# Fused Nyström attention and two feed-forward layers on one Trainium2 core: weight conversions loaded one ahead of their arithmetic, token blocks of the next tile begun two quartets later

## The chip, the core and the metric

The kernel runs on one core of a Trainium2 chip (trn2). The metric is the device time of one launch in microseconds (us). Below, TensorE is called PE, VectorE DVE, ScalarE ACT, GpSimd POOL and SyncE SP, as the profile calls them. All loads and stores of this kernel are issued from SP.

## What is computed

Inputs arrive as 64-bit floats. An attention block with landmarks feeds two feed-forward layers:

```python
A, Bm, C = sm(q, k_lm), sm(q_lm, k_lm), sm(q_lm, k)     # 4 batches, 8 heads, 576 tokens, 32 landmarks
x = (A @ Z @ C @ v)                                     # Z: six Newton steps towards the inverse of Bm
h = x @ w_in;  x = (h * clip(h + 3, 0, 6) / 6) @ w_out  # 2304 tokens, 512 -> 2048 -> 512
h = x @ w2_in; x = elu(h) @ w2_out                      # the same sizes
```

## The kernel before

**Stages.** The first feed-forward layer is worked in 128 slots (`NA`): four batches, two halves of a batch, 16 slices of the hidden width. Slot i multiplies into the hidden slice (`slot_a1`), applies the gate on ACT and DVE, and three slots later multiplies back (`slot_a2`). The attention of the next batch, its matmuls included, is worked between the slots. The second layer is worked in 24 quartets: three tiles of 768 tokens, eight quartets a tile. A quartet has seven block products (`quartet`, the seven blocks stand for eight by a Strassen-like scheme) and the products back to the output (`second`), which follow eight blocks behind.

**Conversions.** The weights of the second layer come as 64-bit floats and must become 32-bit floats before the quartets. That is done by 32 conversions, 16 of `w_out` (`conv_out2`, line 351) and 16 of `w_in` (`conv_in2`, line 354), one in every second slot from slot 36 (`O2`, line 1197). Each calls `to_dram` (line 291): SP loads 512 KB into a tile `u`, ACT makes the number (`y<-u`, line 226) and scales the low word (`u<-u`, line 228), DVE shifts and puts in the sign (`y<-y`, line 232, and `y<-u,y`, line 237), POOL adds the low word (`y<-y,u`, line 241), and SP stores `y` (256 KB) to a scratch buffer in DRAM. `to_dram` issues the load, then `flush` issues the store of the conversion before, then comes the arithmetic. There are three `u` buffers (`UB`) and two `y` buffers (`YB`). The `u` buffers also serve as scratch elsewhere (`scratch`, line 358).

**Token blocks.** For a tile t the second layer needs 14 sums and differences of blocks of the first layer's output, each split into a high and a low part. `load_x(t)` (line 534) is a generator of 24 steps; the loop calls one step per block of a quartet, so that a tile takes 24/7 = 3.4 quartets. For tile 0 it runs in the last slots (line 1202, on DVE), for tiles 1 and 2 it starts in quartet 1 and quartet 9 (`XPACE`, line 1233), with its subtractions on POOL (`xf<-xf,x`, `xf<-x,xf`, `x<-xf,x`, `x<-x`) and its copies on ACT. Its work tiles `xf` take the places of `ath0`, `ath1` and `atl0`, which hold the attention operand of the first layer and later the output rows `ob`.

**Weights of a quartet.** `load_in2` and `load_out2` load the converted weights, split them (`wi<-wi`, `wi<-u,wi`, `w<-w` on POOL; eight small sums and differences `u<-u,wi`, `u<-wi,u` on DVE) and, in the first tile, store the split form for the later tiles.

**What sets the order.** Each engine works its own queue strictly in order. The order in a queue is not that of the program text: a scheduler lays it down when the kernel is built. `wanted(s)` gives the instructions that follow it a due number, counted in slots (a quartet counts as four). `gated` binds the load of a conversion to come, in the schedule, behind the matmuls of the slot before. `flow` keeps the arithmetic of the conversions in their own order on each engine. In the second layer `bmm` fixes the order of the matmuls by hand.

The calls around the change are these:

```python
        if (i - END) % O2 == 0 and conv:
            gate[0] = marks["slot"]
            wanted(i + 4)
            conv.pop(0)()
            gate[0] = None
...
        if q % NQ == XPACE and q // NQ + 1 < NTT:
            xs = load_x(q // NQ + 1, pool)
...
            wanted(NA + 4 * q + 4 * p / 7 + 4)
            if conv and p % 2 == 0:
                conv.pop(0)()
            next(xs, None)
```

Of the kernel before, what the change touches and what calls it, by code (L numbers as in the profile page):

```python
# [10 lines left out]
F32 = mybir.dt.float32  # L11
# [20 lines left out]
def nystrom_ffn_kernel(ctx: ExitStack, tc, q, k, v, w_in1, w_out1, w_in2, w_out2, out):  # L32
# [49 lines left out]
    W = 512  # L82
# [10 lines left out]
    YB, UB, SE = 2, 3, 1  # L93
    PRE, NLEAD, EI, EO = 2, 2, 3, 4
    GATE1, O2, NEW1 = 8, 2, 0
    PACE, NEW, PACE1 = 0.5, -4, 0.2
    XSET, XPACE = 4, 1
    NAT = 25, 28, 31

    strict = [False]  # L100
# [23 lines left out]
    vec, act, pool, pe = InOrder(nc.vector), InOrder(nc.scalar), InOrder(nc.gpsimd), InOrder(nc.tensor)  # L124
# [9 lines left out]
    stg = ctx.enter_context(tc.tile_pool(name="stg", bufs=2, reuse_waits="tile"))  # L134
# [16 lines left out]
    def wanted(s):  # L151
        tc.cur_priority = int(1000 * (s + 100))
# [11 lines left out]
    def gated(inst):  # L164
        if gate[0] is not None:
            after(inst, gate[0])
# [38 lines left out]
    def flow(eng, inst):  # L205

        if not strict[0] and eng.flow is not None:
            after(inst, eng.flow)
        eng.flow = inst.ins

    def steps(src, u, f, out=None):

        if len(src.shape) == 3:
            gated(sp.dma_start(
                out=u.rearrange("p n t -> p (n t)"), in_=src.rearrange("p k n -> p (k n)").bitcast(U32)
            ))
            u = u.rearrange("p (k n) t -> p k n t", k=src.shape[1])
            lo, hi = u[:, :, :, 0], u[:, :, :, 1]  # L220
        else:
            gated(sp.dma_start(out=u.rearrange("p n t -> p (n t)"), in_=src.bitcast(U32)))
            lo, hi = u[:, :, 0], u[:, :, 1]
        fi = f.bitcast(U32)
        yield act, 0
        flow(act, act.activation(out=f, in_=hi.bitcast(F32), func=AF.Copy, scale=2.0 ** -112))
        yield act, 0
        flow(act, act.activation(out=lo, in_=lo, func=AF.Copy, scale=2.0 ** -29))
        yield vec, 1

        t = fi if between[0] is None else between[0].bitcast(U32)
        flow(vec, vec.tensor_scalar(
            out=t, in0=fi, scalar1=3, scalar2=0x7FFFFFFF, op0=ALU.logical_shift_left, op1=ALU.bitwise_and
        ))
        if between[0] is None:
            yield vec, 1
        flow(vec, vec.scalar_tensor_tensor(
            out=fi, in0=hi, scalar=0x80000000, in1=t, op0=ALU.bitwise_and, op1=ALU.bitwise_or
        ))
        yield pool, 1  # L240
        flow(pool, pool.tensor_tensor(out=fi if out is None else out.bitcast(U32), in0=fi, in1=lo, op=ALU.add))

    def run(gen):
        for _ in gen:
            pass
# [32 lines left out]
    def room(tag=None):  # L278
        if tag:
            return nat.tile([128, W, 2], U32, name="un", tag=tag)  # L280
        return stg.tile([128, W, 2], U32, name="u", tag="u", bufs=UB)

    pending = []

    def flush():

        while pending:
            o, i = pending.pop(0)
            sp.dma_start(out=o, in_=i)

    def to_dram(o, src, k=1):

        u = room()
        y = stg.tile([128, W], F32, name="y", tag="y", bufs=YB)
        gen = steps(src, u, y.rearrange("p (k n) -> p k n", k=k) if k > 1 else y)
        next(gen)
        flush()
        run(gen)
        pending.append((o, y))

    def to_pair(f, h, l, eng=vec):
        act.copy(out=h, in_=f)
# [48 lines left out]
    def conv_out2(kk):  # L351
        to_dram(wo2d[kk], part(w_out2, kk, 0))

    def conv_in2(m, kk):

        to_dram(wi2d[m, kk], w_in2[m, kk], 4)
# [321 lines left out]
    def newton(b):  # L678

        EB, sb, sc, cvs = newton_tiles()  # L680
        s = [SB * (b - 1) + (NEW if b > 1 else NEW1)]
        kept = {}

        def go(gen, n=99):
            for _ in range(n):
                wanted(s[0])
                try:
                    s[0] += next(gen) * (PACE if b > 1 else PACE1)
                except StopIteration:
                    return  # L690

        def keep(key, gen):
            kept[key] = yield from gen

        go(prep(b, 0))
        go(score_b(b, 0, sb, EB))
        go(keep(0, score_c(b, 0, sc)))
        go(soft(b, 0))
        go(values(b, 0, kept[0], cvs))
        go(prep(b, 1))  # L700
        go(score_b(b, 1, sb, EB))
        inv = keep("Q", inverse(EB, sb))
        sC = keep(1, score_c(b, 1, sc))
        sA = soft(b, 1)
        go(inv, 1)
        go(sC, 2)
        go(inv, 1)
        go(sC)
        go(inv, 2)
        go(sA, 3)  # L710
        go(inv, 2)
        v1 = values(b, 1, kept[1], cvs)
        go(v1, 2)
        go(inv, 2)
        go(sA)
        go(v1)
        go(inv)
        go(finish(b, kept, cvs, sc))
# [75 lines left out]
    def attn_at(b, hf, eng=pool):  # L794

        s, n = span(b, hf)
        ath = nat.tile([128, G, n], F32R, name="ath", tag=f"ath{hf}")
        atl = nat.tile([128, G, n], F32R, name="atl", tag=f"atl{hf}")
        for g in range(G):
            at = ft.tile([128, T2], F32, name="at", tag="at" if g or b or hf else "gf", bufs=1 if g or b or hf else 2)[:, 0:n]  # L800
            vec.transpose(out=at, in_=e_t[b, g][:, s // 32:(s + n) // 32, :].rearrange("p t l -> p (t l)"))
            yield
            act.copy(out=ath[:, g, :], in_=at)
            sub(atl[:, g, :], at, ath[:, g, :].bitcast(F32), eng)
        at_t[b, hf] = (ath, atl)

    def attn_n(b, c, n=W):

        nh = nat.tile([128, G, W], F32R, name=f"nh{c}", tag=f"nh{c}")
        nl = nat.tile([128, G, W], F32R, name=f"nl{c}", tag=f"nl{c}")  # L810
        n_t[b, c] = (nh, nl)
        w1 = w1_t[b, c]
        mt = mt_t[b]
        for o in range(0, W, n):

            nps = [bank()[:, 0:n] for _ in range(G)]
            for j in range(4):
                for g in range(G):
                    p0 = 64 * g
                    inst = mm(nps[g][32 * j:32 * j + 32, :], mt[p0:p0 + 64, j, :],  # L820
                              w1[p0:p0 + 64, o // 128:(o + n) // 128, j, :], True, True)
                    ordered(inst)
                    if b > 1 and g == j == 0:
                        after(inst, marks["slot"])
                        after(inst, prev[0])
            if b > 1:
                hold[0] = last[0]
            for g in range(G):
                h, l = nh[:, g, o:o + n], nl[:, g, o:o + n]
                act.copy(out=h, in_=nps[g])  # L830
                sub(l, nps[g], h.bitcast(F32))
            yield
        nb, nc_ = (b, c + 2) if c + 2 < NW else (b + 1, c + 2 - NW)
        if 0 < nb < B:
            load_w1(nb, nc_)
# [341 lines left out]
    conv = [lambda kk=kk: conv_out2(kk) for kk in range(NKT)]  # L1177
    conv += [lambda m=m, kk=kk: conv_in2(m, kk) for m in range(NQ) for kk in range(2)]
    for i in range(END, NA):
        b, r = i // SB, i % SB  # L1180

        wanted(i)
        if r == 0:
            run(attn_n(b, NW - 1))
            run(attn_at(b, 1))
            if b + 1 < B:
                newton(b + 1)
            else:
                att.close()
                win.append(ctx.enter_context(tc.tile_pool(name="win", bufs=1, side="right", reuse_waits="tile")))  # L1190
                xp.append(win[0])
                x0 = load_x(0, vec)
        if b + 1 < B and r == NKT:
            run(attn_at(b + 1, 0))
        if b + 1 < B and r in NAT:
            run(attn_n(b + 1, NAT.index(r)))
        if (i - END) % O2 == 0 and conv:
            gate[0] = marks["slot"]
            wanted(i + 4)
            conv.pop(0)()  # L1200
            gate[0] = None
        if i >= NA - SB + XSET:
            wanted(i + 4)
            next(x0, None)
        if i == NA - 14:
            wanted(i + 2)
            load_in2(0)
        wanted(i)
        run(slot_a1(i))
        run(slot_a2(i - DELAY))  # L1210

    def late():

        for i in range(NA - DELAY, NA):
            a2 = slot_a2(i, bmm)
            for _ in range(NDM):
                next(a2)
                yield
            run(a2)

    def seconds():
        for q in range(NTT * NQ):
            yield from second(q)
# [4 lines left out]
    behind, tail, xs, n = seconds(), late(), x0, 0  # L1228
# [59 lines left out]
```

## Time and profile before

| | |
|---|---|
| median of 3 runs | 828.68 us (828.0 to 829.87) |
| the profiled execution: its time | 831.11 us |
| its span, from the first to the last instruction | 829.3 us |
| mean granted TensorE clock | 0.987 |
| conversions: first load issued, last load issued | 160.4 us, 357.1 us |
| quartets of the second layer: sum of the first, of the last | 439.3 us, 803.8 us |

The profile is one execution, recorded by the hardware. Busy time of PE is modelled, since matmuls are pipelined. An idle time is followed by what ended it: "[2.22 <-DMA u<-in_moe_w_out]" means that the engine had been idle for 2.22 us, and that the load landing in `u` ended it. PEclk is the share of the full TensorE clock that was granted. Both weight tensors of one kind have one name in the trace (`in_moe_w_in` is that of either layer).

### The profile page before, as it was taken

To read this page: it belongs to the slowest core of one execution; us is meant where nothing else is said; L and a number is where in the kernel's file an instruction comes from. 1 tells how busy PE (TensorE), PEld (TensorE's weight loads), DVE (VectorE), ACT (ScalarE), POOL (GpSimd) and SP (SyncE) were. 2 spreads that over 40 slices of the span, in tenths; PEclk is the share of its full clock that TensorE was granted. 3 is DMA by queue.
4 is the path that set the end of the run, shared out by engine and by line. 5 is a ranking of instruction groups with operands and counts; after the bars stand their busy time and mean duration, and the time that the engine had idled before them with its cause. 6 is when DMAs were issued, how large, how long until landed. Compare 5 with 4: busy or idle time off the path is not lost.

```text
span 829.3 us, 15433 instructions
## 1 busy us (share of the span) xinstructions
PE 792.0 (96%) x5660; PEld 693.3 (84%) x5660; DVE 508.9 (61%) x1026; ACT 446.5 (54%) x977; POOL 334.4 (40%) x348
## 2 busy tenths in 40 slices
PE   5699999999999999989998999999999999999998
PEld 3476777687887899879998899999988899999996
DVE  7889677547645664387346776756665545545543
ACT  3577554645656666584556555655444434434433
POOL 2466566556645665456428663530470000000000
PEclk9899999999999999999999899999999999999999
DMA  9947932676568544752352476776754654753532
GB/s 336 403 145 232 318 116 87 185 242 210 189 214 256 185 141 158 240 188 102 104 200 78 173 271 233 257 283 245 275 180 142 217 199 178 251 207 139 208 123 77
DMA packets 95564, 165.65 MB, mean 200 GB/s; under 512 B 7232, under 2 KB 51264, under 8 KB 95488
## 3 DMA queue, kind: packets, MB, share of 16 engines
q1 hardware_dynamic: 95488, 164.66, 58.0%
q8 instruction: 45, 0.74, 0.4%
q14 instruction: 31, 0.25, 0.1%
HBM read 119.54 MB, written 45.09 MB: 199 GB/s over the span
## 4 chain that ended last, share of the span: by engine, by line
PE 76%; DVE 9%; DMA 6%; ACT 3%; POOL 3%; issue 2%; SPq 0%; DVEq 0%; POOLq 0%; ACTq 0%
PE x L110 41%; PE h L110 29%; PE bk L110 5%; DMA u<-in_moe_w_out 2%; DVE u L110 1%; DMA qt<-in_q 1%; POOL x L110 1%; DVE y L110 1%; DVE gf L110 1%; DVE nl L110 1%; DVE x L110 1%; DVE lm L110 1%; DVE st L110 1%; DMA u<-in_moe_w_in 1%; ACT nh L110 1%
## 5 line engine op out<-in xcount | busy, mean ns | idle before, releaser
L110 PE MATMUL h<-x,wi 128*128 128x384 f32 x1008 | 205.6, 339 | 0.3 <-DVE y L110 0.3
L110 PE MATMUL x<-gh,wo 128*128 128x288 f32 (+1 forms) x896 | 198.9, 297 | 1.1 <-ACT xs L110 0.7
L110 PEld LDWEIGHTS h<-x,wi 128*128 128x128 f32 x1008 | 182.4, 189 | 13.8 <-DVE y L110 0.8
L110 PEld LDWEIGHTS x<-gh,wo 128*128 128x128 f32 x896 | 149.4, 188 | 11.7 <-issue 7.6
L110 PE MATMUL x<-gl,wo 128*128 128x288 f32 (+1 forms) x448 | 130.7, 294 | 0.0
L110 ACT CAST gh<-gf 128x288 fp32r<-128x288 f32 (+2 forms) x172 | 78.7, 458 | 83.9 <-DVE gf L110 83.6
L110 PE MATMUL x<-w,gh 128*128 128x512 f32 x360 | 116.9, 395 | 1.0 <-ACT gh L110 1.0
L110 POOL TENSOR_TENSOR gl<-gf,gh 128x288 fp32r<-128x288 f32 (+1 forms) x100 | 83.1, 834 | 85.6 <-ACT gh L110 75.6
L110 ACT ACTIVATE gf<-y 128x384 f32<-128x384 f32 x96 | 50.4, 525 | 101.2 <-DVE y L110 101.2
L110 DVE SCALAR_TENSOR_TENSOR gf<-gf,y 128x384 f32<-128x384 f32 x96 | 65.2, 680 | 56.3 <-ACT gf L110 56.3
L110 PE MATMUL x<-w,ghl 128*128 128x512 f32 x324 | 89.1, 392 | 0.0
L110 PE MATMUL h<-atl,nh 128*128 128x288 f32 (+2 forms) x256 | 81.6, 319 | 7.1 <-DVE gf L110 4.3
L110 ACT ACTIVATE gf<-h,half_b 128x288 f32<-128x288 f32 (+2 forms) x128 | 63.6, 499 | 42.2 <-PE h L110 39.4
L110 PEld LDWEIGHTS x<-gl,wo 128*128 128x128 f32 x448 | 84.4, 188 | 1.1 <-issue 0.9
L110 DVE SCALAR_TENSOR_TENSOR gf<-gf,h 128x288 f32<-128x288 f32 (+1 forms) x112 | 49.5, 443 | 55.9 <-ACT gf L110 55.0
L110 PEld LDWEIGHTS x<-w,gh 128*128 128x128 f32 x360 | 67.8, 190 | 10.6 <-ACT gh L110 1.4
L110 PE MATMUL h<-ath,nl 128*128 128x288 f32 (+2 forms) x256 | 76.4, 299 | 0.0
L110 PE MATMUL h<-ath,nh 128*128 128x288 f32 (+2 forms) x256 | 76.1, 297 | 0.0
L110 PE MATMUL x<-w,gl 128*128 128x512 f32 x180 | 71.6, 398 | 3.6 <-DVE gl L110 3.6
L110 PEld LDWEIGHTS x<-w,ghl 128*128 128x128 f32 x324 | 60.2, 188 | 8.4
L110 PEld LDWEIGHTS h<-atl,nh 128*128 128x128 f32 x256 | 48.3, 189 | 20.5 <-DVE gf L110 7.7
L110 DVE TENSOR_TENSOR gl<-gf,gh 128x384 fp32r<-128x384 f32 (+1 forms) x72 | 45.8, 636 | 23.0 <-ACT gh L110 18.5
(151 smaller groups left out, 1269.4 us busy)
## 6 DMA issues: line engine op xcount, KB each, us to landing
wi<-wi2p SPq DMA_DIRECT2D x64, 448.0 KB, 4.8
w<-wo2p SPq DMA_DIRECT2D x32, 512.0 KB, 5.7
wi2p<-wi SPq DMA_DIRECT2D x32, 448.0 KB, 2.9
u<-in_moe_w_in SPq DMA_DIRECT2D x25, 512.0 KB, 5.1
w1c<-w1d SPq DMA_DIRECT2D x48, 256.0 KB, 4.3
ub<-in_moe_w_out SPq DMA_DIRECT2D x16, 512.0 KB, 10.3
u<-in_moe_w_out SPq DMA_DIRECT2D x16, 512.0 KB, 5.0
wo2p<-w SPq DMA_DIRECT2D x16, 512.0 KB, 3.3
```

What stands on the lines that cost most here:

```text
L110: inst = getattr(self.eng, name)(*a, **kw)
```

## The change

`to_dram` now issues the load of its conversion, then the pending stores, and then does the arithmetic of the conversion before (`convert`); its own arithmetic follows in the next call. The tile `y` is taken when the arithmetic begins (`place`), no longer ahead of the load. After the last conversion its arithmetic follows at once. A store is issued two calls behind its load, formerly one. `XPACE` goes from 1 to 3.

```diff
-    XSET, XPACE = 4, 1
+    XSET, XPACE = 4, 3
...
+        yield act, 0
+        f = f() if callable(f) else f
         fi = f.bitcast(U32)
-        yield act, 0
         flow(act, act.activation(out=f, in_=hi.bitcast(F32), func=AF.Copy, scale=2.0 ** -112))
...
+    loaded = []
+
     def to_dram(o, src, k=1):
-        u = room()
-        y = stg.tile([128, W], F32, name="y", tag="y", bufs=YB)
-        gen = steps(src, u, y.rearrange("p (k n) -> p k n", k=k) if k > 1 else y)
+        y = []
+
+        def place():
+            y.append(stg.tile([128, W], F32, name="y", tag="y", bufs=YB))
+            return y[0].rearrange("p (k n) -> p k n", k=k) if k > 1 else y[0]
+
+        gen = steps(src, room(), place)
         next(gen)
         flush()
-        run(gen)
-        pending.append((o, y))
+        convert()
+        loaded.append((gen, o, y))
+
+    def convert():
+        while loaded:
+            gen, o, y = loaded.pop(0)
+            run(gen)
+            pending.append((o, y[0]))
...
             conv.pop(0)()
+            if not conv:
+                convert()
             gate[0] = None
```

## Rows read from the trace of the kernel before

**Rows 1.** The page: busy time and share of each engine, whole span.

```profile
PE 792.0 (96%) x5660; PEld 693.3 (84%) x5660; DVE 508.9 (61%) x1026; ACT 446.5 (54%) x977; POOL 334.4 (40%) x348
```

**Rows 2.** The page: the chain that ended last, by engine.

```profile
PE 76%; DVE 9%; DMA 6%; ACT 3%; POOL 3%; issue 2%; SPq 0%; DVEq 0%; POOLq 0%; ACTq 0%
```

**Rows 3.** Waits of ACT, 160 to 366 us: idle us in total, times, longest.

```profile
ACT y L110 <- DMA u<-in_moe_w_out: 14.2, 8, 3.6
ACT y L110 <- DMA u<-in_moe_w_in: 13.4, 9, 3.0
```

**Rows 4.** Windows: stretch, us, busy of PE, PEld, DVE, ACT, POOL, clock, DMA, GB/s.

```profile
160.00:365.00 205.00, 200.32 (x1872) 174.60 (x1864) 117.00 (x265) 123.23 (x287) 115.40 (x127) 0.99 0.64 206
186.00:194.00 8.00, 6.15 (x31) 3.84 (x30) 6.78 (x20) 5.47 (x13) 4.06 (x4) 0.79 0.82 268
...
447.00:458.00 11.00, 6.46 (x33) 5.57 (x33) 10.36 (x15) 6.83 (x16) 8.29 (x8) 0.92 0.39 123
456.00:463.00 7.00, 5.42 (x14) 4.73 (x15) 5.09 (x9) 2.54 (x5) 6.64 (x6) 0.51 0.33 131
...
480.00:543.00 63.00, 63.00 (x316) 57.10 (x315) 44.55 (x93) 38.58 (x76) 34.01 (x26) 1.00 0.71 257
```

**Rows 5.** Timeline of PE: the stalls at 189, 269 and 355 us.

```profile
188.97 0.40 PE L110 MATMUL h<-atl,nh 128*128 128x288 f32 x1 [1.85 <-DVE gf L110]
...
268.86 0.40 PE L110 MATMUL x<-gh,wo 128*128 128x288 f32 x1 [0.70 <-ACT xs L110]
...
354.75 1.69 PE L110 MATMUL bk<-w1c,mt 64*32 64x512 f32 x16 [1.17 <-DVE nl L110]
```

**Rows 6.** Timeline of ACT: conversions that waited for their load.

```profile
186.03 0.67 ACT L110 ACTIVATE y<-u 128x512 f32<-128x512 f32 x1 [2.22 <-DMA u<-in_moe_w_out]
...
351.48 0.67 ACT L110 ACTIVATE y<-u 128x512 f32<-128x512 f32 x1 [2.97 <-DMA u<-in_moe_w_in]
```

**Rows 7.** Timeline of SP: start, us taken by the issue, what is issued.

```profile
178.19 0.33 SPq L110 DMA_DIRECT2D w<-wo2d  x1
...
208.84 0.37 SPq L110 DMA_DIRECT2D u<-in_moe_w_out  x1
213.06 0.33 SPq L110 DMA_DIRECT2D wo2d<-y  x1
...
219.09 0.33 SPq L110 DMA_DIRECT2D wo2d<-y  x1
219.52 0.37 SPq L110 DMA_DIRECT2D u<-in_moe_w_out  x1
```

**Rows 8.** Timeline of POOL: first and last step of tile 1's token blocks.

```profile
434.75 1.30 POOL L110 TENSOR_TENSOR xf<-xf,x 128x384 f32<-128x384 f32 x1 [9.54 <-PE h L110]
...
469.59 1.01 POOL L110 TENSOR_TENSOR x<-xf,x 128x384 fp32r<-128x384 f32 x1 [3.35 <-ACT x L110]
```

**Rows 9.** Timeline of DVE: the sum of quartet 1's second block.

```profile
454.77 0.55 DVE L110 TENSOR_TENSOR u<-h,a 128x384 f32<-128x384 f32 x1
```

**Rows 10.** Timeline of PE: the stall at 457 us.

```profile
457.58 0.79 PE L110 MATMUL x<-w,gl 128*128 128x512 f32 x1 [3.58 <-DVE gl L110]
```

**Rows 11.** Tiles u and xf: count, ns min/median/max, first and last start.

```profile
L110 DVE TENSOR_TENSOR u<-h,a x24: 544/557/559, 439.3 to 803.8; 128x384 f32<-128x384 f32 x24
...
L110 DVE TENSOR_TENSOR u<-u,wi x32: 279/292/1095, 375.5 to 534.9; 128x128 f32<-128x128 f32 x32
...
L110 SPq DMA_DIRECT2D u<-in_moe_w_out x16: 372/401/592, 160.4 to 260.3; - x16
...
L110 POOL TENSOR_TENSOR x<-xf,x x16: 1010/1085/1341, 439.3 to 618.5; 128x384 fp32r<-128x384 f32 x16
```

**Rows 12.** Timeline of POOL: the weight splits of one quartet.

```profile
488.85 2.63 POOL L110 TENSOR_TENSOR wi<-wi 128x384 fp32r<-128x384 f32 x2 [6.85 <-DVE u L110]
491.43 2.56 POOL L110 TENSOR_TENSOR wi<-u,wi 128x512 fp32r<-128x512 f32 x2
493.93 3.19 POOL L110 TENSOR_TENSOR w<-w 128x512 fp32r<-128x512 f32 x2
```

**Rows 13.** Timeline of SP: tile 2's first token load; its last.

```profile
549.11 0.85 SPq L110 DMA_DIRECT2D x<-x1d  x2
...
604.34 0.33 SPq L110 DMA_DIRECT2D xf<-x1d  x1
```

**Rows 14.** Windows: tile 2's token blocks on POOL; columns as in rows 4.

```profile
591.00:621.00 30.00, 29.67 (x147) 26.34 (x147) 20.58 (x29) 16.27 (x34) 25.27 (x22) 1.00 0.57 200
```

## The prediction

> **What bounds the kernel now.** I read the busy times first [rows 1]: PE is busy for 792.0 of the 829.3 us span, the next engine, DVE, for 61%. A change elsewhere pays only where PE stands still or runs at a lower clock. The chain of waits says the same [rows 2]: 76% of it is PE, 6% DMA. So I looked for PE's lost time in the two stretches that the edits touch, by windows [rows 4].
>
> In the stretch of the conversions (160 to 365 us) PE is idle for 205.0 - 200.3 = 4.7 us. Three stalls make up 1.85 + 0.70 + 1.17 = 3.7 us of it [rows 5]. ACT's own waits for conversion loads are far longer, 14.2 + 13.4 = 27.6 us in 17 waits [rows 3], but nearly all of that is ACT's spare time: it is busy for 123.2 of the 205 us. Only a wait that makes a gate or a copy behind it late reaches PE. The waits at 186 and 351 us [rows 6] end 3 us ahead of the PE stalls at 189 and 355 us, and fit such a chain. The stall at 189 us is followed by a lower clock: 0.79 on average from 186 to 194 us, which over 6.15 us of PE work is 6.15 x 0.21 = 1.3 us more.
>
> At the turn from slots to quartets PE is idle for 11.0 - 6.5 = 4.5 us (447 to 458 us), of which one wait is 3.58 us [rows 10], and the clock then stands at about half (0.51, 456 to 463 us): 5.42 x 0.49 = 2.7 us. Together 7.2 us. In that stretch DVE is busy for 10.4 of 11 us. From 480 to 543 us PE has no idle time at all.
>
> **What sets the order.** Both edits move work in the program text and in its due number, so the question is what these decide. The trace says: hardly anything, where the work is ready earlier. The first half-weight for quartet 0 is loaded at 178.2 us [rows 7], and the text issues that load in quartet 0, whose first sum is at 439.3 us [rows 11]. Tile 2's first token load is issued at 549.1 us [rows 13]. A quartet takes (803.8 - 439.3)/23 = 15.85 us [rows 11], so that is (549.1 - 439.3)/15.85 = 6.9 quartets in, where the text has it in quartet 9. And two stores stand in a row at 213.1 and 219.1 us, between the loads at 208.8 and 219.5 us [rows 7], where the text alternates load and store. The scheduler fills an engine with whatever is ready; the due number only chooses between things ready at once.
>
> **The change, part by part.**
>
> *Arithmetic one call later.* Each of the 32 conversions keeps its load, its gate and its five arithmetic instructions. No instruction is added. The due number of the arithmetic grows by two slots, which is (260.3 - 160.4)/15 = 6.7 us [rows 11]. But the arithmetic becomes ready when its load lands, and it was already the work with the latest due number on its engines at that time (four slots ahead of the slot in hand, against the slots' own gates and the attention). So ACT's queue gets it at the same place, and ACT waits for the same loads as before. Lower bound: nothing. Upper bound, if all of it moves behind the landing: the three stalls and the clock, 3.7 + 1.3 = 5.0 us gained. I take near zero, by the rows of what sets the order.
>
> *Stores one call later.* 32 issues of 0.33 us on SP [rows 7] stay 32. A store is ready when POOL has added, and then SP is mostly free. Where a store and the next load are ready together, the load now goes first, 0.33 us earlier. Reaching one of the three stalls, that is 0.3 us gained; reaching none, nothing. I take 0.3. The last two stores now have the due number of the end of the slots. SP is dense there with the first tile's loads, but the data of the last conversion is wanted in quartet 7 only, some 7 x 15.85 = 111 us later: nothing, and what covers it is that distance.
>
> *Buffers.* A load one ahead can hold a second `u`, and there are three. Nothing, as long as the arithmetic stays where it is. If it were held back, the load two calls on would wait for POOL to free its buffer: that belongs to the slower end of the range.
>
> *Token blocks two quartets later.* The 24 steps, their eight loads, 22 POOL operations and 14 ACT copies per tile stay. For tile 1 the first POOL step starts at 434.75 us after waiting 9.54 us for PE [rows 8], which had to finish with the attention operand whose place it takes; the last step starts at 469.6 us. In the text the steps run from quartet 1 to the middle of quartet 4. Quartet 1's second block is summed at 454.8 us [rows 9], so the first step ran before quartet 1 and the last at about its end. It ran as early as its buffer allowed, and POOL was free. A due number eight slots later changes neither. Tile 2 likewise: its loads came ahead of the text, then waited for the buffers of the output rows until past 587 us, its last load being at 604.3 us [rows 13]; the burst on POOL from 591 to 621 us costs PE 30.0 - 29.7 = 0.3 us [rows 14]. Bounds: 7.2 + 0.3 = 7.5 us gained if tile 1's blocks do leave the turn; on the other side the collision priced below. I take zero.
>
> **Sum.** 0 - 0.3 + 0 = -0.3 us on the profiled execution's 831.1 us (span 829.3 and 1.8 around it). That execution is 2.4 us above the median of 828.7 us; against the median the forecast is 828.4 us.
>
> **The rivals.**
>
> *The loads do run ahead (0.18).* If the scheduler honours the later due number, ACT's 27.6 us of waits go and with them the three stalls and the clock: 828.7 - 5.0 = 823.7 us. For it: the waits are there, and two of them sit right before PE stalls. Against it: the rows of what sets the order. The Trainium skill (Trainium Kernel Development and Optimization, Best Practices) asks for double buffering so that transfers overlap compute; by that rule the time would be this rival's. The trace has the overlap already, and its waits are a matter of place in the queue.
>
> *Tile 1's blocks leave the turn (0.12).* Then POOL is free while DVE makes the sums of the weights, and the 7.2 us are gained: 821.5 us, with the first rival 816.5 us. For it: DVE's small sums take 292 ns in the middle and up to 1095 ns [rows 11], the long ones at the turn.
>
> *Tile 1's blocks meet the weight splits: slower (0.14).* If the due number does hold them back, they come into quartets 3 to 6. There POOL has 2.63 + 2.56 + 3.19 = 8.4 us of splits in each quartet [rows 12], and 22 operations of 1.085 us [rows 11] over 3.4 quartets add 7.0 us: 15.4 of 15.85 us. The gaps of POOL are where DVE makes its eight sums, so the stall of the turn, 3.58 us, could come in each of four quartets: 14.3 us, less the 7.2 gained at the turn: 828.7 + 7.1 = 835.8 us. It decides if more than two quartets stall so (2 x 3.58 = 7.2). The Trainium skill (SBUF — State Buffer, Who interferes with whom) says that a DVE operation with two inputs in SBUF and a GpSimd operation that reads SBUF block one another for a whole instruction. The long sums agree: 1095 ns is about one POOL operation of 1010 to 1341 ns.
>
> *A few places are exchanged (0.16).* Ties decided otherwise move a gate behind another wait. One stall like that at 189 us with its clock is 1.85 + 1.3 = 3.2 us either way: 825.5 or 831.9 us, the gain taken at 0.06 and the loss at 0.10.
>
> **How the numbers follow.** The forecast, no visible change, has 0.40; about 0.2% (1.7 us) is what a measurement of this kernel can tell from none. Faster: 0.18 + 0.12 + 0.06 = 0.36; slower: 0.14 + 0.10 = 0.24. The range reaches from 821 us, which takes in the first rival and the second alone, to 834 us, which takes in the exchange and most of the collision; both gains together and the collision in four quartets are left out. The likeliest case's own range is 827.0 to 830.4 us.
>
> **What would show it.** Right: ACT's waits for the loads of `u` again near 28 us; SP's loads and stores in the same sequence; POOL's first token step of tile 1 again right after the slots, near 435 us; PE's stalls at 189 and 457 us still there. Wrong: ACT's waits near zero and no stall at 189 us (first rival); the first POOL token step after 470 us, and then either a turn without the 3.58 us stall (second) or PE idle in quartets 3 to 6, where it had none (third).

## The result, and the profile after

The changed kernel takes 833.91 us (median of 8 runs, 831.22 to 836.75) where the kernel before takes 828.64 us (median of 8, 827.69 to 830.52). The ratio is 1.0059, with a 95% interval from 1.0043 to 1.0075: slower by 0.6%. The forecast was no visible change. The time lies inside the range, on the side that got 0.24.

The profiled execution after took 833.99 us, with a span of 832.2 us. Its first lines answer to [rows 1] and [rows 3]. The page of the kernel after, busy time and share of each engine:

```profile
PE 794.2 (95%) x5660; PEld 694.6 (83%) x5660; DVE 505.5 (61%) x1026; ACT 446.4 (54%) x977; POOL 333.2 (40%) x348
```

Waits of ACT of the kernel after, 160 to 366 us (idle us in total, times, longest):

```profile
ACT y L110 <- DMA u<-in_moe_w_in: 13.2, 9, 2.7
ACT y L110 <- DMA u<-in_moe_w_out: 12.4, 8, 3.3
```

The same instructions are there, with nearly the same busy time (PE 794.2 us against 792.0). ACT waits for the conversions' loads for 25.6 us, where it waited 27.6 us. So the arithmetic did not move behind its loads. Tile 1's token blocks did not move either. POOL takes them up as soon as PE lets go of the buffer, and the turn has its stall as in [rows 8] and [rows 10], only 3.2 us later. Timeline of POOL of the kernel after, the first token step of tile 1:

```profile
438.21 1.08 POOL L110 TENSOR_TENSOR xf<-xf,x 128x384 f32<-128x384 f32 x1 [10.03 <-PE h L110]
```

Timeline of PE of the kernel after, the stall of the turn:

```profile
460.78 0.50 PE L110 MATMUL x<-w,gl 128*128 128x512 f32 x1 [3.56 <-DVE gl L110]
```

So neither edit did what its words say, and yet the kernel is slower. I looked for the first place where the two executions part. Set side by side, the instructions of every engine's queue stand in the same order up to about 358 us. The first difference is on SP. Timeline of SP of the kernel before (start, us taken by the issue, what is issued):

```profile
355.64 0.32 SPq L110 DMA_DIRECT2D wi2d<-y  x1
...
357.07 0.35 SPq L110 DMA_DIRECT2D u<-in_moe_w_in  x1
358.58 0.32 SPq L110 DMA_DIRECT2D wi2d<-y  x1
359.31 0.32 SPq L110 DMA_DIRECT2D u<-x1d  x1
```

The same of the kernel after:

```profile
355.66 0.35 SPq L110 DMA_DIRECT2D u<-in_moe_w_in  x1
356.18 0.32 SPq L110 DMA_DIRECT2D u<-x1d  x1
...
357.74 1.42 SPq L110 DMA_DIRECT2D x<-x1d  x3
359.22 0.43 SPq L110 DMA_DIRECT2D wi<-wi2d  x1
361.07 0.32 SPq L110 DMA_DIRECT2D wi2d<-y  x1
```

The load of the last conversion (`u<-in_moe_w_in`) is followed before by the store of the last conversion but one, and then by further token loads of the first tile (`u<-x1d`, `x<-x1d`). After, the store comes behind seven other issues, 5.41 us behind that load instead of 1.51. These token loads follow the load 1.7 us sooner, and the first sums and casts of tile 0 come into other places on DVE and ACT. Timeline of DVE before:

```profile
362.97 0.43 DVE L110 TENSOR_SCALAR y<-y 128x512 uint32<-128x512 uint32 x1 [1.71 <-ACT y L110]
363.43 0.69 DVE L110 SCALAR_TENSOR_TENSOR y<-u,y 128x512 uint32<-128x512 uint32 x1
364.04 1.16 DVE L110 TENSOR_TENSOR u<-u,x 128x384 f32<-128x384 f32 x1
365.13 0.44 DVE L110 SCALAR_TENSOR_TENSOR gf<-gf,h 128x288 f32<-128x288 f32 x1
```

Timeline of DVE after:

```profile
361.52 0.56 DVE L110 TENSOR_TENSOR u<-u,x 128x384 f32<-128x384 f32 x1 [1.72 <-DMA u<-x1d]
361.99 0.42 DVE L110 TENSOR_SCALAR y<-y 128x512 uint32<-128x512 uint32 x1
...
364.34 0.68 DVE L110 SCALAR_TENSOR_TENSOR y<-u,y 128x512 uint32<-128x512 uint32 x1
...
367.00 0.44 DVE L110 SCALAR_TENSOR_TENSOR gf<-gf,h 128x288 f32<-128x288 f32 x1
```

Before, one token operation stands between the conversion and the gate (`gf<-gf,h`), and the gate starts 1.4 us after its ACT part (363.72 us). After, the token sums are mixed with the conversion, and the gate starts 3.2 us after its ACT part (363.79 us). On ACT three casts of token and weight tiles (362.55 to 363.79 us) now go ahead of that gate and of the copies `xs`. Timeline of ACT before, the gate's ACT part:

```profile
363.72 0.51 ACT L110 ACTIVATE gf<-h,half_b 128x288 f32<-128x288 f32 x1
```

Timeline of ACT after:

```profile
362.55 0.51 ACT L110 CAST x<-x 128x384 fp32r<-128x384 f32 x1
362.97 0.50 ACT L110 CAST x<-u 128x384 fp32r<-128x384 f32 x1
363.38 0.51 ACT L110 CAST wi<-wi 128x384 fp32r<-128x384 f32 x1
363.79 0.49 ACT L110 ACTIVATE gf<-h,half_b 128x288 f32<-128x288 f32 x1
```

PE waits for gates and copies. Timeline of PE before, all stalls of 358 to 400 us:

```profile
365.62 0.40 PE L110 MATMUL h<-atl,nh 128*128 128x288 f32 x1 [1.08 <-DVE gf L110]
...
373.34 0.40 PE L110 MATMUL h<-atl,nh 128*128 128x288 f32 x1 [0.59 <-DVE gf L110]
...
382.57 0.40 PE L110 MATMUL h<-atl,nh 128*128 128x288 f32 x1 [0.78 <-DVE gf L110]
```

The same after:

```profile
364.62 0.40 PE L110 MATMUL x<-gh,wo 128*128 128x288 f32 x1 [1.49 <-ACT xs L110]
...
367.50 0.40 PE L110 MATMUL h<-atl,nh 128*128 128x288 f32 x1 [0.70 <-DVE gf L110]
...
371.23 0.40 PE L110 MATMUL h<-atl,nh 128*128 128x288 f32 x1 [0.55 <-DVE gf L110]
...
375.16 0.40 PE L110 MATMUL h<-atl,nh 128*128 128x288 f32 x1 [0.23 <-DVE gf L110]
...
381.07 0.40 PE L110 MATMUL h<-atl,nh 128*128 128x288 f32 x1 [1.95 <-DVE gf L110]
...
385.12 0.40 PE L110 MATMUL h<-atl,nh 128*128 128x288 f32 x1 [1.40 <-DVE gf L110]
```

Three stalls of 2.45 us in all became six of 6.32 us, 3.9 us more. PE's own queue has another order too from there on (its first difference is the `x<-gh,wo` at 364.62 us, where `h<-atl,nh` came before), and POOL's from 375 us. So the stalls come from all the exchanged places together, and this trace does not tell their shares. Two marks give the whole loss of this stretch: the issue of the last conversion's load and POOL's first token step of tile 1, which waits for the last slots. Between them lie 434.75 - 357.07 = 77.7 us before and 438.21 - 355.66 = 82.6 us after. That is 4.9 of the 5.3 us between the medians; 1 us of it is in no gap that the trace shows.

Why did the store move? The text of the change issues a store two calls behind its load. The store of conversion 30 (counted from 0) was formerly issued in the call of conversion 31, with that slot's due number. Now that call issues the store of conversion 29, and conversion 30's is left to the last `flush` behind all slots (line 1225 of the kernel before). Its due number is then that of the end of the slots, where it was 102 (four slots ahead of slot 98). The first tile's token loads, issued from slot 100 on, have numbers between the two, so where they are ready together with the store, they now go first.

### The profile page after: what moved, and what is told of

Same layout as the page of the kernel before. It is cut to its first block, busy times and chain, and to the rows that moved or that the text cites. A ratio compares the mean times of both kernels' runs of the same rounds, so it can differ in the third digit from the quotient of the medians.

```text
span 832.2 us, 15433 instructions
## 1 busy us (share of the span) xinstructions
PE 794.2 (95%) x5660; PEld 694.6 (83%) x5660; DVE 505.5 (61%) x1026; ACT 446.4 (54%) x977; POOL 333.2 (40%) x348
## 4 chain that ended last, share of the span: by engine, by line
PE 75%; DVE 8%; DMA 7%; ACT 4%; POOL 3%; issue 2%; SPq 0%; POOLq 0%; DVEq 0%; ACTq 0%
PE x L110 40%; PE h L110 29%; PE bk L110 6%; DMA u<-in_moe_w_in 3%; DVE u L110 2%; DVE y L110 1%; POOL x L110 1%; DMA out<-ob 1%; DMA kt<-in_k 1%; DVE gf L110 1%; DVE lm L110 1%; DVE nl L110 1%; DVE st L110 1%; DMA u<-in_moe_w_out 1%; POOL xf L110 1%
## 5 line engine op out<-in xcount | busy, mean ns | idle before, releaser
L110 ACT CAST gh<-gf 128x288 fp32r<-128x288 f32 (+2 forms) x172 | 78.7, 457 | 79.8 <-DVE gf L110 79.4
L110 DVE SCALAR_TENSOR_TENSOR gf<-gf,y 128x384 f32<-128x384 f32 x96 | 61.5, 642 | 59.5 <-ACT gf L110 59.5
L110 PEld LDWEIGHTS x<-w,gh 128*128 128x128 f32 x360 | 67.3, 189 | 10.4 <-ACT gh L110 1.4
```

Source lines behind the costliest of these rows:

```text
L110: inst = getattr(self.eng, name)(*a, **kw)
```

## The experiments

**The theory** is that this one store makes the whole loss. **Its rivals** are that the arithmetic or the token blocks make it by places that I had not seen, or that the loss is spread over many exchanged places. The ratios below are to runs of the kernel before taken together with each kernel, on the same chip.

### The store alone, taken back and put in

The first kernel is the changed one with the store of conversion 30 issued where it was:

```diff
             if not conv:
+                flush()
                 convert()
```

> The kernel after, with one line more: the pending store (that of the last conversion but one) is issued ahead of the last conversion's arithmetic, with the due number that it had in the kernel before. All loads stay one ahead of their arithmetic in the text, the tokens two quartets later. Theory 1 (that one store): back to 828.6 us, within 0.2%; PE stalls between 358 and 390 us back from 6.3 to 2.5 us. Rival 1 (the arithmetic of the conversions, two slots later in due number, costs the time): it stays near 833.9 us.

Measured: 829.66 us against 828.95, ratio 1.0004 [0.9987, 1.0021]. The queues of all engines have the order of the kernel before, and PE's stalls of 358 to 400 us come to 2.71 us.

The second is the kernel before, with nothing but that store moved:

```diff
         u = room()
...
-        flush()
+        if conv:
+            flush()
         run(gen)
```

> The kernel before, with one store moved: the last conversion does not flush, so that the store of the one before it is issued at the end of the slots. Nothing of the two edits is in it. Theory 1: 833.9 us, slower by 0.4 to 0.8%, with PE stalls of some 6.3 us between 358 and 390 us. Rival 1 (arithmetic) and rival 2 (token blocks): 828.6 us.

Measured: 834.44 us against 828.95, ratio 1.0067 [1.0046, 1.0088]. The queues have the order of the changed kernel on every engine. PE has five stalls of 4.65 us in all between 358 and 400 us, where the changed kernel has six of 6.32 us, and a granted clock of 0.96 there, where the changed kernel has 1.00: (42.0 - 4.7) x 0.04 = 1.5 us more, so that the two lose about as much. Timeline of PE of this kernel, the first and the last of the five:

```profile
363.43 0.40 PE L110 MATMUL x<-gh,wo 128*128 128x288 f32 x1 [1.53 <-ACT xs L110]
...
379.55 0.57 PE L110 MATMUL h<-atl,nh 128*128 128x288 f32 x1 [1.95 <-DVE gf L110]
```

One issue of 0.32 us, made some 4 us later, makes all of the loss, and both edits without it make none. This is shown from both sides.

### The token blocks alone

```diff
-    XSET, XPACE = 4, 1
+    XSET, XPACE = 4, 3
```

> The second edit alone: XPACE 3 in the kernel before, nothing else. Theory 1 (all of the 5.3 us come from one store, that of the last conversion but one, which now has the due number of the end of the slots and goes behind tile 0's token loads on SP): 828.6 us, within 0.2%, and tile 1's first POOL step again near 435 us. Rival 2 (the token blocks of tile 1 meet the weight splits): most of the loss is here, 832 us or more, and PE idle after 470 us.

Measured: 828.86 us against 828.95, ratio 0.9997 [0.9975, 1.0019]. Not one instruction stands in another place. So this kernel gives a second profile of the order of before, and it tells which stalls belong to that order. Timeline of PE, 358 to 400 us:

```profile
362.85 0.40 PE L110 MATMUL h<-atl,nh 128*128 128x288 f32 x1 [1.14 <-DVE gf L110]
...
370.57 0.40 PE L110 MATMUL h<-atl,nh 128*128 128x288 f32 x1 [0.59 <-DVE gf L110]
...
379.80 0.40 PE L110 MATMUL h<-atl,nh 128*128 128x288 f32 x1 [0.78 <-DVE gf L110]
```

They are the three stalls of before, 2.51 us in all against 2.45. The stall at 189 us [rows 5] isn't in this execution. Nor is it in that of the changed kernel, whose queues have the same order up to there.

### One place put back

Which of the exchanged places costs? This kernel has the late store, but binds tile 0's first sum on DVE behind the last conversion:

```diff
-            sub(f[1], f[0], l[0], eng)
+            first = sub(f[1], f[0], l[0], eng)
+            if t == 0 and kk == 0:
+                after(first, eng.flow)
```

> The kernel before with the store of the last conversion but one moved behind the token loads, as in one_store_late, and with one place put back: the first tile's first token sum on DVE follows the last conversion's two DVE operations again, as before the change. On ACT two casts still stand ahead of a gate (three in one_store_late), and on DVE the first gate behind the conversion still has four token operations ahead of it, where it has one in the kernel before. If the exchange of sum and conversion at the front of DVE's queue made the loss, the ratio to the kernel before is 0.998 to 1.002 and PE's stalls from 358 to 400 us come to 2 to 3 us. If the casts ahead of the gate and the sums ahead of the gates made it, the ratio stays at 1.004 to 1.008 and the stalls at 5 to 7 us. Between the two (1.002 to 1.004), both have a share.

Measured: 831.75 us against 829.45, ratio 1.0022 [1.0005, 1.0040], between the two. PE's stalls of 358 to 400 us come to 4.0 us. With the front of DVE's queue put back, more than half of the loss goes, by the medians; the interval is wide. The store itself is still late, with the same seven issues ahead of it. What of the rest is ACT's casts ahead of a gate, what is DVE's sums ahead of the next gate and what is PE's own order, the run does not separate. Two of its six stalls (0.47 and 0.45 us) wait for POOL's `gl`, which no stall of the changed kernel does.

The two marks, the last conversion's load and the first token step of tile 1, agree with the times:

| kernel | load, us | token step, us | between | ratio of the times |
|---|---|---|---|---|
| before | 357.07 | 434.75 | 77.7 | |
| token blocks alone | 354.22 | 431.97 | 77.8 | 0.9997 |
| store taken back | 359.77 | 438.02 | 78.3 | 1.0004 |
| one place put back | 354.17 | 434.44 | 80.3 | 1.0022 |
| store alone | 354.41 | 436.67 | 82.3 | 1.0067 |
| after | 355.66 | 438.21 | 82.6 | 1.0059 |

The two kernels of the last experiment below have the order of before up to 431 us, 3 us ahead of the second mark, and their marks are 77.7 and 78.8 us apart. So one order spreads by about 1 us here.

### The arithmetic really held back

The edit's words promise that arithmetic no longer waits for its load. To see what that is worth, the changed kernel with the store taken back binds each conversion's first ACT instruction behind the slot in whose call it stands:

```diff
-        flow(act, act.activation(out=f, in_=hi.bitcast(F32), func=AF.Copy, scale=2.0 ** -112))
+        first = act.activation(out=f, in_=hi.bitcast(F32), func=AF.Copy, scale=2.0 ** -112)
+        gated(first)
+        flow(act, first)
...
             if not conv:
+                flush()
                 convert()
```

> The kernel of the run before the last (the store put back), and in it the first ACT operation of each conversion is bound behind the matmuls of the slot ahead of the call in which it stands in the text, so that it does come one conversion later. This is what the first edit says. If ACT's waits for the loads cost PE what the prediction's upper bound has: ACT's waits for u fall from 27.6 us to under 5 us, the stalls at 189, 269 and 355 us go, and the time is about 823.7 us. If those waits are ACT's spare time: the waits go and the time stays within 0.3% of 828.6 us. If the order at the end of the slots decides: it moves by some us either way with the stalls between 355 and 400 us.

Measured: 833.94 us (829.85 to 840.42) against 828.95, ratio 1.0065 [1.0036, 1.0094]. Waits of ACT, 160 to 366 us:

```profile
ACT y L110 <- DMA u<-in_moe_w_out: 6.1, 3, 3.3
...
ACT y L110 <- DMA u<-in_moe_w_in: 4.6, 2, 3.3
```

Now most of the arithmetic does what the edit says: 10.7 us of waits instead of 27.6, where under 5 us was expected. The time does not fall. PE's idle time from 160 to 358 us, 198.0 - 194.5 = 3.5 us, lies between those of before and of the token blocks alone, which have one and the same order (4.2 and 1.8 us). Its marks are 353.50 and 436.27, 82.8 us apart: it loses at the place where the changed kernel loses, and the stalls there are like those (timeline of PE):

```profile
367.96 0.40 PE L110 MATMUL h<-atl,nh 128*128 128x288 f32 x1 [1.96 <-DVE gf L110]
...
383.17 0.40 PE L110 MATMUL h<-atl,nh 128*128 128x288 f32 x1 [1.40 <-DVE gf L110]
```

The last conversions now come later, into tile 0's token sums. And the store of conversion 30, though it is issued in the text where it was, is ready later (its last DVE part ends at 357.8 us), and falls behind the same seven issues on SP as in the changed kernel (359.37 us, 5.9 us behind the load). So this kernel has the late store again, and its median says nothing of the arithmetic alone. The profiled execution (829.85 us) is also the fastest of its ten. The spread of its times is wider than that of any other kernel here; why, stays open.

### The token blocks really held back

The same for the second edit: the kernel before with `XPACE` 3 and the loads of tiles 1 and 2 bound behind the last block product issued in the text (`chain[0]`):

```diff
-                sp.dma_start(out=o, in_=x1d[2 * r + kk, :, t0 + c * T2:t0 + c * T2 + T2])
+                load = sp.dma_start(out=o, in_=x1d[2 * r + kk, :, t0 + c * T2:t0 + c * T2 + T2])
+                if t:
+                    after(load, chain[0])
```

> The kernel before with XPACE 3, and each token load of tiles 1 and 2 bound, in the schedule, behind the second layer's matmul that stands just before it in the text. So the blocks do begin in quartets 3 and 11, as the second edit says. Rival 2 of the prediction (the turn is freed): POOL's first step of tile 1 after 490 us, PE's idle time from 447 to 458 us down from 4.5 us to under 1 us and no lower clock behind it, time about 821.5 us. Rival 3 (they meet the weight splits): PE idle in quartets 3 to 6, where it had none, 3.6 us for each quartet hit; 832 us or more. If the stall at the turn has another cause than POOL: about 828.6 us, with the 3.6 us stall still there.

Measured: 833.48 us against 829.78, ratio 1.0043 [1.0028, 1.0057]. Windows of this kernel (stretch, us, busy of PE, PEld, DVE, ACT, POOL, clock, DMA, GB/s):

```profile
447.00:458.00 11.00, 10.26 (x54) 8.94 (x53) 9.21 (x19) 7.29 (x17) 5.25 (x4) 1.00 0.47 161
...
480.00:543.00 63.00, 56.14 (x262) 49.30 (x261) 48.56 (x81) 38.72 (x81) 49.11 (x42) 0.95 0.63 221
```

The turn is free: PE busy for 10.3 of 11 us instead of 6.5, at the full clock [rows 4]. But from 480 to 543 us, where PE had no idle time, it is idle for 6.9 us, and the clock is 0.95. Timeline of PE there:

```profile
490.14 1.35 PE L110 MATMUL h<-x,wi 128*128 128x384 f32 x6 [2.40 <-DVE u L110]
...
525.90 2.29 PE L110 MATMUL h<-x,wi 128*128 128x384 f32 x6 [2.60 <-DVE u L110]
```

Two shorter ones, of 0.75 us at 485.25 us and 1.11 us at 535.26 us, stand beside them.

POOL at that time (timeline of this kernel):

```profile
482.35 2.00 POOL L110 TENSOR_TENSOR xf<-x,xf 128x384 f32<-128x384 f32 x2 [1.07 <-DMA x<-x1d]
```

And DVE:

```profile
483.39 2.12 DVE L110 TENSOR_TENSOR u<-u,wi 128x128 f32<-128x128 f32 x2 [1.69 <-POOL xf L110]
...
486.44 0.28 DVE L110 TENSOR_TENSOR u<-u,wi 128x128 f32<-128x128 f32 x1
```

DVE's sums take 1.06 us each beside a POOL operation and 0.28 us when POOL is between two: the third rival's collision, moved from the turn into the quartets. The Trainium skill (SBUF — State Buffer, Who interferes with whom) says that a DVE instruction with two inputs in SBUF contends with a GpSimd instruction that reads SBUF. This trace agrees: 1.06 us beside POOL, 0.28 us without it.

### Tile 0 held, and everything held

If token loads coming too early make the loss, holding tile 0's loads should take it away. The changed kernel, with tile 0's loads (in `load_x`, line 913 of the kernel before) bound behind the matmuls of the slot that issues them:

```diff
+                if t == 0:
+                    after(load, marks["slot"])
```

> The kernel after (both edits, store late), with each token load of tile 0 bound behind the matmuls of the slot in whose step it stands, so that the blocks of tile 0 are spread from slot 100 on and no longer follow the conversions as a burst. If the loss of the change is those blocks getting ahead of the slots' gates on DVE and ACT: the PE stalls between 358 and 390 us (6.3 us) fall to under 2 us and the time is below 829 us though the store is still late. If the late store costs by itself: it stays at 834 us. If the blocks are only moved to where they do the same harm: the stalls stand later, 400 to 440 us, and the time is 829 to 834 us.

Measured: 831.78 us against 829.78, ratio 1.0027 [1.0013, 1.0041]. The marks are 356.21 and 434.91, 78.7 us apart: the loss of the stretch shrinks to 1 us, with stalls of 1.65 us at 363.7 us and 1.77 us at 403.3 us. The time comes down by less than that would give; the rest I can't place. With the token loads out of its way the store goes at once, 0.5 us behind the last conversion's load (356.68 after 356.21 us), though its due number is the late one. So the run fits the theory that the two compete for the place on SP, but it does not show what early token loads alone would cost.

The kernel before with the loads of all tiles held, and `XPACE` 2:

> The kernel before with the token loads of all tiles bound behind their matmuls, those of tiles 1 and 2 from quartets 2 and 10 on (XPACE 2). If the gains add: stalls of 2.5 us at 358 to 390 us and of 7.2 us with the clock at the turn gone, 819 to 823 us. If tile 1's blocks at quartet 2 collide with the weight splits: over 828.6 us.

Measured: 834.0 us against 829.78, ratio 1.0058 [1.0035, 1.0080]. The collision comes sooner and is spread thinner: PE is idle for 63.00 - 59.55 = 3.45 us between 480 and 543 us, most of it one stall of 2.35 us at 510 us, and has stalls of 1.23 and 0.32 us at 473 and 478 us. Two more stand in tile 0's stretch (1.71 us at 364.9, 1.76 us at 404.5 us). From 358 to 543 us PE is idle for 9.3 us, before for 7.1 us; that is half of the 4.2 us between the medians, and the rest isn't placed.

The changed kernel with the store back, the arithmetic held, the loads of all tiles held and `XPACE` 2, so that every step runs where the text has it:

> As the run before, and the arithmetic of the conversions held one call back as well (with the store put back). If ACT's waits for conversion loads cost PE something: 2 to 5 us below the run before. If they are spare time: within 0.2% of it.

Measured: 833.17 us against 829.78, ratio 1.0041 [1.0016, 1.0065]. This is the arithmetic's own test, since the kernel above differs from it by the conversions alone: 833.17 against 834.0 us, 0.1% apart. ACT's waits are 10.4 us here too (6.4 and 4.0). So the waits were mostly spare time: the scatter of these runs (829.67 to 837.65) leaves room for a gain of 2 or 3 us, but not for the 5.0 us of the prediction's upper bound. None of the held kernels so far beats the kernel before, though each shortens the wait that it is aimed at.

### The turn cleared without the collision

The turn was priced at 7.2 us. Holding all of tile 1's blocks gives it back in the quartets. So I left the first half of tile 1's blocks where it runs, before the turn, and held only the second half, to the second block of quartet 1, by when the first splits are done:

```diff
+                if t == 1 and kk == 1:
+                    after(load, chain[0])
...
-        if q % NQ == XPACE and q // NQ + 1 < NTT:
+        if q % NQ == (XPACE if q < NQ else 1) and q // NQ + 1 < NTT:
...
-            next(xs, None)
+            for _ in range(2 if q == 0 and p < 3 else 1):
+                next(xs, None)
```

(`XPACE` is 0, all else is the kernel before. Without the last edit the second half falls to the fifth block of quartet 1: the second kernel.)

> The kernel before (no edit of the change), and only the second half of tile 1's token blocks held: its four loads are bound behind the matmul of quartet 1's second block, so that POOL does quartet 2's weight splits first and the second half in the gap after them. The run with all of tile 1 held showed the turn freed (lost PE time from 440 to 460 us 1.4 us against 6.4 us) and two new stalls of 5.5 us in quartets 2 and 5, when the blocks ran beside DVE's sums for the weights. If those stalls come only from this overlap, and the gap of POOL from 463 to 473 us takes the second half: the turn is freed and no new stall comes, 822 to 825 us. If the second half still overlaps with the next quartet's sums: one stall of 3.6 to 5.5 us in quartet 2, 828 to 830 us.

> As the run before, with the second half held three blocks longer, to quartet 1's fifth block. Its POOL work then meets quartet 3's weight splits and DVE's sums for them. Overlap theory: one stall of 3.6 to 5.5 us in quartet 2 in place of that at the turn, 827 to 830 us, slower than the run before by 3 us or more. If overlap is not what costs: the same time as the run before.

Measured: the first 826.43 us against 829.71, ratio 0.9957 [0.9937, 0.9976], faster than both kernels, by less than the 822 to 825 us expected; the second 830.38 us, ratio 1.0010 [0.9993, 1.0027]. Windows of the first (columns as above):

```profile
440.00:480.00 40.00, 37.11 (x198) 33.60 (x197) 31.33 (x53) 24.23 (x53) 32.08 (x29) 1.00 0.46 157
447.00:458.00 11.00, 9.87 (x52) 8.63 (x51) 9.29 (x21) 7.87 (x18) 4.66 (x5) 1.00 0.67 211
480.00:543.00 63.00, 63.00 (x315) 56.98 (x314) 45.71 (x95) 39.05 (x79) 34.47 (x25) 1.00 0.73 267
```

Windows of the second, 440 to 480 us:

```profile
440.00:480.00 40.00, 35.09 (x164) 30.52 (x163) 31.67 (x52) 23.59 (x51) 27.85 (x23) 0.91 0.56 193
```

In the first, the turn has PE at work for 9.9 of 11 us and the clock stays up, and the quartets from 480 us on are full as before. The gain is 3.3 us of the 7.2. One stall is left, 1.76 us at 473.9 us, where the second half's last steps meet quartet 2's splits. In the second, a stall of 3.18 us at 470.3 us and a mean clock of 0.91 over the stretch cost about what the turn had cost. Measured from quartet 0's first sum, POOL begins the second half at 459.17 - 440.15 = 19.0 us in the first kernel and at 458.44 - 435.16 = 23.3 us in the second, and the next weights' sums on DVE begin at 466.67 - 440.15 = 26.5 and 463.18 - 435.16 = 28.0 us. Timeline of DVE of the second kernel:

```profile
463.18 2.12 DVE L110 TENSOR_TENSOR u<-u,wi 128x128 f32<-128x128 f32 x2
465.22 1.08 DVE L110 TENSOR_TENSOR u<-wi,u 128x128 f32<-128x128 f32 x1
...
468.85 1.35 DVE L110 TENSOR_TENSOR ghl<-gf,ghl 128x384 fp32r<-128x384 f32 x1
```

The first four sums are long there, and all eight stand ahead of the operand `ghl` that PE waits for, which takes 1.35 us itself. In the first kernel three of the first four are long, and `ghl` (469.95 us, 0.55 us) comes after the fourth. A shift of 4.3 us decides it, by the gap into which the blocks fall; how much of it is the collision and how much the place of `ghl` in DVE's queue is not separated.

## Why the prediction was wrong

**What bounds the kernel, and what sets the order: right.** PE is busy for 95% of the span, and what moved the time is what PE waits for. The due number only chooses between things ready at once: but for one store, no instruction that the edits name changed its place.

**Arithmetic one call later: right at zero, but the upper bound was not there to gain.** ACT's waits stayed (25.6 us). I had bounded the gain by three stalls and a low clock, 5.0 us. The kernel with `XPACE` 3 alone has the same order and no stall at 189 us: PE's idle time from 160 to 358 us was 198.0 - 193.8 = 4.2 us in the profile of before and 198.0 - 196.2 = 1.8 us in that one. The stall at 189 us, the longest of the three, comes and goes with the execution: the kernel with the store taken back, again of the same order, has 1.12 us at that place, and its low clock (0.79, 196 to 204 us) stands behind another stall. And when most of the waits really went (10.7 and 10.4 us left), no gain of that size came.

**Stores one call later: the step that failed.** It said of the last two stores, which get the due number of the end of the slots: "nothing, and what covers it is that distance", the 111 us until the data is wanted. That prices the store by the reader of its data. The store of conversion 30 is also a place in SP's queue, ahead of the token loads. Giving up that place let the token loads go earlier, and with them the places on DVE and ACT were chosen anew, ahead of gates that PE waits for. The term came to +4.9 us between the two marks and +5.3 us in the medians. The text had the due number right and the loads standing there too ("SP is dense there"); it did not ask who moves up when the store steps back.

**Token blocks two quartets later: right at zero**, ratio 0.9997, and the first token step again right after the slots.

**The rivals.** *The loads run ahead* did not happen. Forced, its 5.0 us are not to be seen: in the first such kernel the late store is there again and costs what the changed kernel lost, while PE's idle time ahead of it (3.5 us) is within what one order shows; in the pair with all loads held the arithmetic changes the time by 0.1%. The rule of double buffering from the Trainium skill (Trainium Kernel Development and Optimization, Best Practices) would have had this rival's time; these runs, where most of the waits are gone, show no such gain. *The blocks leave the turn* did not happen. Forced, it frees the turn as priced (PE idle for 0.7 us between 440 and 480 us instead of 4.5, the clock at 1.00 instead of 0.91), and loses it again elsewhere. Its rows placed the long DVE sums at the turn; four of 0.8 to 1.4 us also stand at 377 to 380 us before, in the last slots. *The blocks meet the splits* did not happen. Forced, it comes, in fewer places than the four quartets taken, with stalls of 2.40 and 2.60 us as the longest, where 3.58 us were taken; the net is +3.7 us, where +7.1 was worked out. *A few places are exchanged* is what happened. It was priced by one stall at 189 us with its clock (3.2 us) and had 0.10 on the slower side. The mechanism was right, its place and size were not: six stalls at 364 to 385 us instead of three, and +5.3 us. Nothing in the prediction tied it to the store.

**The signs.** Two of the signs for "right" held (ACT's waits, POOL's first step), and so did the stall at 457 us. The stall at 189 us is gone from the execution after, which the prediction took as a sign of the first rival; but it is gone from the kernel with the blocks alone as well, which has the order of before, so that sign tells nothing. The one that broke and counts was "SP's loads and stores in the same sequence": same for 358 us, then not. That was the sign to look at, and the sequence could have been worked out from the text beforehand: with one call of `flush` fewer behind it, a store is carried past everything that was due in between.

## What to carry to other kernels

Where a scheduler lays down the order, a moved DMA issue has two prices: when its data is wanted, and who moves up in its queue when it steps back. The second can be the larger, and it is read at the ends of a pipeline, where the last items fall out of the loop's pattern and take the due number of whatever follows. Where a wait is only spare time of an engine off the critical path, removing it gains little or nothing; and work taken off a crowded place pays only if it lands in a gap, so look for the gap before moving it.

## What was not expected of the hardware

With one and the same order of instructions, PE's stalls under the conversions differ from execution to execution. The kernel before, the one with the blocks alone and the one with the store taken back have the same queues; the two that clear the turn have them up to 431 us. In these five profiles PE is idle from 160 to 358 us for 4.2, 1.8, 5.7, 4.9 and 1.8 us, while the stalls of 358 to 400 us come to 2.45, 2.51, 2.71, 2.52 and 3.24 us. So the times of single executions of the kernel before spread over some 7 us (825.5 to 832.2 in 27 runs), and a stall that one profile shows is no safe base for a bound until a second execution of the same order has it too.
